# Attention and expert layer on one core: the weights and rows of the left-over steps

## The chip, the cores and the metric

The kernel runs on one core of a Trainium2 chip. The metric is device time in microseconds (us), the median of the timed runs. TensorE (PE) multiplies, ScalarE (ACT), VectorE (DVE) and GpSimd (POOL) do the elementwise work, and SyncE (SP) issues most of the transfers; POOL issues the gathers and scatters of single rows.

## The reference, cut to what matters

```python
# attention: q 4 x 12288 x 128; kv pooled 4x4 into 768 keys per batch, k = v
a = softmax(q @ k.T / sqrt(C));  x = a @ v
# expert layer over all 49152 rows, 8 experts, 128 -> 1024 -> 128
logits = x @ w_gate;  e = argmax(logits);  g = softmax(logits)[e]
y = g * (relu(x @ w1[e]) @ w2[e])
```

Every row goes through the one expert that its gate picks.

## The kernel before, in words

The rows are cut into 96 blocks of 512. Neighbouring blocks form groups, and each group picks by vote the expert that most of its rows want; its blocks then run through that expert in full. Rows whose expert is another one are left over. They are done again at the end in left-over steps of 128 rows (`TAIL`), one expert and one batch to a step. Two such steps (`EXTRA`) are laid out at compile time; a loop on the device (line 1476) takes any that are still missing, and here it runs no time.

A block's expert layer runs in eight parts f of 128 hidden units. `hidden(job, f)` makes three matmuls into one of three PSUM banks m, ACT writes the high half hh (line 549, Relu) and DVE the low half hl (line 555); a bank is free again when hl is there. `combine(job, f)` adds three matmuls with w2 into a bank y, three parts behind (`DEEP`). When a block is done, ACT copies y out as 16-bit planes (line 588), a transposing transfer turns them, and POOL joins and scales them (lines 594 and 598).

Most of the kernel is ordered by hand (`by_hand`). From the last eight blocks on a planner orders the instructions: of those that are ready on an engine by its model it takes the one that stands earliest in the program. `pin` keeps an instruction from passing those that the program has before it on its engine.

In that last stage each part f of a block is followed by one call of `search()`, which advances each left-over step by one piece, up to its next `yield`. Such a stretch is a slice here. The pieces of `tail_step`, in order: the loads of the expert's raw weights, of the batch's keys, values and units (piece 3); finding the 128 rows (pieces 3 to 7); gathering their q (piece 8, line 928, POOL); the maxima of the two raw weights in `weight_scales` (line 495) and their spread over the partitions by a small matmul; then `split_expert` for each weight: wh on ACT (line 523), the raw weight scaled in place on ACT (line 525), wl = raw - wh in two halves on POOL (line 528). Then q's rows are scaled, turned on PE (line 947) and halved (lines 344 and 345), and `scores` makes the six score matmuls, the row maximum (line 361), the exponentials (line 368), their high half (line 391), their low half (line 393, POOL) and a transposing transfer into aT (line 394, SP). After a number of empty pieces `values` multiplies aT with the values (18 matmuls, the first pinned), x is halved (lines 404 and 409), and the gate gives the rows' factors (`scale`). The second step begins one slice after the first has set `found`, which is when its scales are there.

Counted in slices from the first step's start, before the change the first step has its scores in slice 18, its exponentials' transfer in 19 and its values in 28. It sets `found` in 12, so the second step has the same pieces twelve slices later: scores in 30, transfer in 31, values in 40. Slices 1 to 40 are the eight parts each of blocks 91 to 95; what is left after 40 has no part of a block between.

The two steps then run as one last job of 256 rows. Each part f has matmuls for either step; their sums lie in two banks of one tile s. `tail_rows` scales both in one instruction (line 991) and scatters each step's rows with an indirect transfer from POOL (line 994).

Of the kernel before, what the change touches and what calls it, by code (L numbers as in the profile page):

```python
# [13 lines left out]
BF16 = mybir.dt.bfloat16  # L14
I32 = mybir.dt.int32
U16 = mybir.dt.uint16
AF = mybir.ActivationFunctionType
ALU = mybir.AluOpType
AX = mybir.AxisListType

P = 128
# [13 lines left out]
TAIL = 128  # L35
# [5 lines left out]
def attention_moe(ctx: ExitStack, tc, q, kv, w_sr, w_gate, w1, w2, out, tail=True):  # L41
    nc = tc.nc
    B, N, C = q.shape
    H, W = kv.shape[1], kv.shape[2]
    E, F = w_gate.shape[1], w1.shape[2]
    NF = F // P
# [17 lines left out]
    NL = B * E  # L64
    BANKS = 3
    DEEP = 3
    LAG = NBG + 4
    WIDE = LAG + 1
    NJ = NBLK * CH
    TC = TAIL // P  # L70
    assert TC == 1 and NJ * P == B * N
    scale = 1.0 / math.sqrt(C)
# [23 lines left out]
    part = persist.tile([P, 1], F32, name="part")  # L96
# [24 lines left out]
    one = sb.enter_context(tc.tile_pool(name="one", bufs=1))  # L121
    two = sb.enter_context(tc.tile_pool(name="two", bufs=2))
    four = sb.enter_context(tc.tile_pool(name="four", bufs=4))
    three = sb.enter_context(tc.tile_pool(name="three", bufs=3))
    xp = sb.enter_context(tc.tile_pool(name="xp", bufs=LAG))
    EXPERTS = {name: sb.enter_context(tc.tile_pool(name=f"ps_{name}", bufs=1, space=bass.MemoryType.PSUM))
# [19 lines left out]
    def mm(o, l, r, start, stop):  # L146
        return nc.tensor.matmul(o, l, r, start=start, stop=stop)  # L147
# [25 lines left out]
    def pin(ins):  # L173

        return ins if by_hand[0] else tc.keep_in_program_order(ins)
# [160 lines left out]
    def q_tiles(wide):  # L336
        if wide:
            return *(four.tile([P, BLK], F32R, name="qh") for _ in range(2)), None
        qhl = four.tile([P, 2, BLK], F16, name="qh")
        return qhl[:, 0], qhl[:, 1], None  # L340

    def q_halves(qT, n, low, qs=None):
        qh, ql, units = q_tiles(qs is None)
        nc.scalar.copy(qh[:, :n * P], qT[:, :n * P])
        low.tensor_sub(ql[:, :n * P], qT[:, :n * P], qh[:, :n * P])
        return qh, ql, units if qs is None else [qs[:, 1, c:c + 1] for c in range(n)]
# [139 lines left out]
        yield  # L486
        nc.vector.reciprocal(gt, gt)

    def weight_scales(raw, to, where):

        ws = one.tile([P, 8], F32, name="ws", bufs=3)
        wm = one.tile([P, 2], BF16, name="wm", bufs=3)
        to.append(ws)
        for i in range(2):
            pin(nc.vector.tensor_reduce(
                wm[:, i:i + 1], raw[i], axis=AX.X, op=ALU.max, apply_absolute_value=True))
            yield
        pw = where()
        pin(mm(pw[:, :2], ones_q, wm, True, True))
        yield  # L500

        pow2(ws[:, 2:4], pw[:, :2])
        nc.vector.reciprocal(ws[:, 4:6], ws[:, 2:4])
        nc.vector.tensor_scalar_mul(ws[:, 4:5], ws[:, 4:5], W1_TOP / Q_TOP)
        nc.vector.tensor_scalar(ws[:, 6:7], ws[:, 2:3], ws[:, 3:4], Q_TOP / W1_TOP, op0=ALU.mult, op1=ALU.mult)
# [6 lines left out]
                          w2[bass.ds(reg, 1)].rearrange("o (f p) c -> p (o f) c", p=P))  # L512
        return r1, r2

    def split_expert(raw, ws, w, i, aside):

        if aside:
            wh, wl = (kvp.tile([P, F], F16, name="kv_raw") for _ in range(2))
        else:
            wh = two.tile([P, F], F16, name=("w1h", "w2h")[i])  # L520
            wl = two.tile([P, F], F16, name=("w1l", "w2l")[i])
        w += [wh, wl]
        nc.scalar.activation(wh, raw[i], AF.Copy, scale=ws[:, 4 + i:5 + i])
        yield
        nc.scalar.activation(raw[i], raw[i], AF.Copy, scale=ws[:, 4 + i:5 + i])
        yield
        for s in (slice(0, F // 2), slice(F // 2, F)):
            nc.gpsimd.tensor_sub(wl[:, s], raw[i][:, s], wh[:, s])

    def job_parts(job):  # L530

        parts = job.get("parts", [job])
        n = job["n"] // len(parts)
        return [(part, slice(i * n, (i + 1) * n), n) for i, part in enumerate(parts)]
# [11 lines left out]
    def hidden_high(job, f):  # L546
        n, (ph,) = job["n"], job["h"][f]
        hh = one.tile([P, BLK], F16, name="hh", bufs=DEEP + 2)
        nc.scalar.activation(hh[:, :n], ph[:, :n], AF.Relu)  # L549
        job["h"][f] = [ph, hh]  # L550

    def hidden_low(job, f):
        n, (ph, hh) = job["n"], job["h"][f]
        hl = one.tile([P, BLK], F16, name="hl", bufs=DEEP + 2)
        nc.vector.scalar_tensor_tensor(hl[:, :n], ph[:, :n], 0.0, hh[:, :n], op0=ALU.max, op1=ALU.subtract)  # L555
# [4 lines left out]
        hidden_high(job, f)  # L560
        hidden_low(job, f)

    def combine(job, f):
        h = job["h"].pop(f)
        fs = slice(f * P, (f + 1) * P)
        for i, (part, cs, n) in enumerate(job_parts(job)):
            w = part["w"]
            if n == TAIL:
                py = job["py"][:, i, :C] if "parts" in job else job["py"][:, :C]
                mm(py, h[0][:, cs], w[2][:, fs], f == 0, False)  # L570
                mm(py, h[1][:, cs], w[2][:, fs], False, False)
                mm(py, h[0][:, cs], w[3][:, fs], False, f == NF - 1)
                continue
            py = job["py"][:, :n]
            mm(py, w[2][:, fs], h[0][:, cs], f == 0, False)
            mm(py, w[2][:, fs], h[1][:, cs], False, False)
            mm(py, w[3][:, fs], h[0][:, cs], False, f == NF - 1)
# [224 lines left out]
    def moe_step(job, f, last):  # L802

        if f < DEEP and last:
            finish(last, f, f + 1)
        hidden(job, f)

        late = {} if "parts" in job else {DEEP: (), DEEP + 1: (0, 1)}
        for i in late.get(f, (f - DEEP,) if f >= DEEP else ()):
            moe_second(job, i)  # L810

    def moe_second(job, f):
        if f == 0:
            job["py"] = SCORES["s"].tile([P, 2, 512], F32, name="s") if "parts" in job else (
                EXPERTS["y"].tile([P, 512], F32, name="y"))
        combine(job, f)

    def finish(job, lo=0, hi=DEEP):
        for f in range(NF - DEEP + lo, NF - DEEP + hi):
            moe_second(job, f)  # L820
        if hi == DEEP and job["n"] == BLK and all(job is not j for j in jobs[-2:]):
            job["yT"] = y_planes(job["py"])
        elif hi == DEEP and job["n"] == BLK:
            job["y"] = y_out(job)
# [55 lines left out]
    def tail_step(job, place, aside=False):  # L880
# [7 lines left out]
        raw = load_expert(reg_e)  # L888
# [43 lines left out]
        yield  # L932
        w = job["w"] = []
        to = []
        for _ in weight_scales(raw, to, bank):
            yield
        ws = to[0]
        job["found"] = True
        for i in range(2):
            for _ in split_expert(raw, ws, w, i, aside):  # L940
                yield
        qs = q_rows(q_sb, TC)
        q_unit_scores(qs, k)
# [2 lines left out]
        for c in range(TC):  # L946
            pin(nc.tensor.transpose(pq[:, c * P:(c + 1) * P], q_sb[:, c, :], ident))
        qhl = q_halves(pq, TC, nc.vector, qs)
        yield
        sums = one.tile([P, TC], F32, name="sums_t", bufs=2)  # L950
        aT = three.tile([P, 2 * KT, BLK], F16, name="aT")
        for c in range(TC):
            s = scores(qhl, c, k, sums[:, c:c + 1], aT)
# [4 lines left out]
            for _ in s:  # L958
                pass
            yield  # L960
        for _ in range(8):
            yield
        po = bank()
        for t in range(KT):
# [6 lines left out]
        to = []  # L971
# [3 lines left out]
        rs, _, gt, _ = to  # L975
# [9 lines left out]
            next(s, None)  # L985

    def tail_rows(job):
        n = job["n"] // TAIL
        o = two.tile([P, CH, C], F32, name="o")
        py = job["py"][:, :n, :C] if "parts" in job else job["py"][:, :C].unsqueeze(1)  # L990
        nc.vector.tensor_tensor(o[:, :n], py, job["scale"].unsqueeze(2).to_broadcast([P, n, C]), op=ALU.mult)
        writes = []
        for i, part in enumerate(job.get("parts", [job])):
            writes.append(nc.gpsimd.indirect_dma_start(  # L994
                out=out, out_offset=bass.IndirectOffsetOnAxis(ap=part["row"], axis=0),
                in_=o[:, i, :], in_offset=None, bounds_check=B * N - 1, oob_is_err=False).ins)
        for i, write in enumerate(writes):
            for before in writes[:i]:
                tc.declare_no_dep(write, before, reason="a token is in one step alone: the rows are others")
# [114 lines left out]
    jobs = [BL[m] if isinstance(m, int) else m for m in order]  # L1114
# [21 lines left out]
    LEN, SHORT = 18.7, 9.8  # L1136
    FIRST = LAG * (LEN - SHORT)
    events, count = [], [0]

    def at(time, part, *args):  # L1140
        heapq.heappush(events, (time, count[0], part, args))
        count[0] += 1
# [9 lines left out]
    def begin(t):  # L1152
        return FIRST + t * SHORT if t < LAG else t * LEN

# [33 lines left out]
    def plan_short(t):  # L1188

        T, z, y = begin(t), t - 2, t - 3  # L1190
        by_pe = t < LAG - 1
        for c, time in enumerate((0.0, 2.55, 6.05, 8.55)):
# [12 lines left out]
        if z >= 0:  # L1205

            last = t == LAG - 1
            at(T + 4.75, block_values, z, range(0, 2))
# [141 lines left out]
    with tc.manual_schedule():  # L1350
# [12 lines left out]
        for t in range(LAG, NBLK):  # L1363
            m, z, T = t - LAG, t - 2, t * LEN
            job, last = jobs[m], jobs[m - 1] if m else None
# [59 lines left out]
    for t in range(NBLK, LAG + len(jobs)):  # L1425
# [36 lines left out]
        if votes is not None and tail and closes(NBLK - 1) == votes:  # L1462
# [3 lines left out]
                job["to"] = jobs[-1]["scale"][:, i * TC:(i + 1) * TC]  # L1466
            places = tail_places(steps_f[:, :EXTRA], EXTRA)
            waiting += [(job, tail_step(job, places[i], aside=i > 0)) for i, job in enumerate(extra)]
    finish(jobs[-1])
    write_rows(order[-1])  # L1470
    if not tail:
        return
# [3 lines left out]
    with tc.For_i(0, n_steps, 1):  # L1476
        job = dict(n=TAIL)
# [32 lines left out]
```

## Time and profile before

| | us |
|---|---|
| median of 3 timed runs | 1863.18 (1863.13 to 1863.6) |
| the profiled execution | 1862.85 |
| its span, first to last instruction | 1861.1 |

| engine | busy us | share of the span |
|---|---|---|
| PE | 1820.6 | 98% |
| DVE | 1438.9 | 77% |
| POOL | 1392.6 | 75% |
| ACT | 1375.9 | 74% |

Busy times are sums over the span; a matmul's end is modelled, so that neighbouring matmuls overlap in the rows. Idle time stands in square brackets behind the instruction that it precedes, with what ended it.

### The profile page before, as it was taken

What the parts mean: (1) busy time and instruction counts of PE and PEld (TensorE: products, weight loads), DVE (VectorE), ACT (ScalarE), POOL (GpSimd) and SP (SyncE); (2) the same over time, 40 slices, a digit from 0 to 9 for tenths busy, and PEclk for the clock granted to TensorE, in tenths of its full rate; (3) what the DMA queues carried; (4) which work ended last, traced back from release to release, by engine and by line L of the source; (5) the groups of instructions that cost most, each with busy time, mean ns of one, the idle gap of its engine ahead of it and who ended that gap; (6) DMA issues with size and microseconds to landing.
All of it is one profiled execution on the core that took longest, in us unless ns stands there. A gap on an engine that the chain in (4) does not pass through costs nothing. (4 is left out here: it accounts for less than half of the span.)

```text
span 1861.1 us, 30957 instructions
## 1 busy us (share of the span) xinstructions
PE 1820.6 (98%) x9959; PEld 925.2 (50%) x9959; DVE 1438.9 (77%) x3016; ACT 1375.9 (74%) x2432; POOL 1392.6 (75%) x1521
## 2 busy tenths in 40 slices
PE   6999999999999999999999999999999999999998
PEld 6654444444454544444444444544444444444444
DVE  6887877887788787777787878877777677787586
ACT  3777867777877878877777777787777786877665
POOL 2769788778878878778688797787786877777643
PEclk9999999999999999999999999999999999999999
DMA  6988889777988987778878887777787777776552
GB/s 185 175 157 161 185 162 180 156 128 161 192 176 155 184 161 131 154 149 151 166 152 186 161 171 150 140 152 153 131 157 149 131 145 150 138 148 138 97 144 55
DMA packets 994837, 284.74 MB, mean 153 GB/s; under 512 B 900432, under 2 KB 979922, under 8 KB 994672
## 3 DMA queue, kind: packets, MB, share of 16 engines
q1 hardware_dynamic: 994544, 282.65, 77.7%
q8 instruction: 79, 1.29, 0.3%
q14 instruction: 86, 0.70, 0.1%
q0 software_dynamic: 128, 0.10, 0.0%
HBM read 80.42 MB, written 28.45 MB: 59 GB/s over the span
## 5 line engine op out<-in xcount | busy, mean ns | idle before, releaser
L393 POOL TENSOR_TENSOR ah<-a,ah 128x768 f16<-128x768 f32 x379 | 622.2, 1649 | 184.5 <-ACT ah L391 137.6
L549 ACT ACTIVATE hh<-m 128x512 f16<-128x512 f32 x776 | 459.5, 593 | 353.7 <-PE m L147 349.3
L555 DVE SCALAR_TENSOR_TENSOR hl<-m,hh 128x512 f16<-128x512 f32 x776 | 526.9, 680 | 166.3 <-ACT hh L549 160.0
L147 PE MATMUL s<-k_sb,qh 128*128 128x384 f16 (+1 forms) x2316 | 448.1, 329 | 10.0 <-ACT a L368 6.9
L361 DVE TENSOR_REDUCE nmax<-s 128x1 f32<-128x768 f32 x386 | 367.8, 953 | 41.9 <-PE s L147 28.7
L368 ACT ACTIVATE a<-s,nmax,qs 128x768 f32<-128x768 f32 x348 | 346.7, 996 | 49.7 <-DVE qs L152 21.2
L147 PE MATMUL m<-aT,v_sb 128*128 128x512 f16 x1584 | 370.6, 379 | 0.0
L147 PE MATMUL m<-xh,w1h 128*128 128x512 f16 x776 | 292.1, 376 | 3.4 <-DVE hl L555 3.4
L147 PEld LDWEIGHTS <-qh 128*128 128x128 f16 x2100 | 205.3, 98 | 175.6 <-DVE qs L152 3.9
L147 PE MATMUL m<-xh,w1l 128*128 128x512 f16 x776 | 292.5, 377 | 0.0
L147 PE MATMUL m<-xl,w1h 128*128 128x512 f16 x776 | 292.4, 377 | 0.0
L147 PE MATMUL y<-hh,w2h 128*128 128x512 f16 x768 | 290.8, 379 | 0.7 <-ACT y L588 0.7
L147 PE MATMUL y<-hl,w2h 128*128 128x512 f16 x768 | 291.1, 379 | 0.3 <-DVE hl L555 0.3
L147 PE MATMUL y<-hh,w2l 128*128 128x512 f16 x768 | 291.1, 379 | 0.0
L147 PEld LDWEIGHTS <-v_sb 128*128 128x128 f16 x1764 | 169.9, 98 | 201.9 <-issue 1.8
L147 PEld LDWEIGHTS <-w2h 128*128 128x128 f16 x1536 | 149.5, 98 | 180.4 <-issue 1.0
L147 PEld LDWEIGHTS <-w1h 128*128 128x128 f16 x1552 | 135.4, 97 | 120.7 <-issue 12.2
L389 POOL CAST ah<-a 128x768 f16<-128x768 f32 x185 | 152.7, 826 | 48.6 <-ACT a L368 46.4
L391 ACT CAST ah<-a 128x768 f16<-128x768 f32 x194 | 161.8, 834 | 2.0
L594 POOL COPY o<-yT 128x512 uint16<-128x512 uint16 x190 | 136.3, 764 | 33.8 <-DMA yT<-y 33.7
L409 DVE SCALAR_TENSOR_TENSOR xl<-m,xs,xh 128x512 f16<-128x512 f32 x88 | 66.1, 751 | 116.8 <-ACT xh L404 115.3
L653 POOL TENSOR_TENSOR qh<-qT,qh 128x512 f16<-128x512 f32 (+1 forms) x95 | 111.2, 1170 | 31.2 <-ACT qh L648 31.1
(252 smaller groups left out, 2044.5 us busy)
## 6 DMA issues: line engine op xcount, KB each, us to landing
kv_raw<-in_moe_w_dram SPq DMA_DIRECT2D x54, 512.0 KB, 4.8
out_dram<-o SPq DMA_DIRECT2D x96, 256.0 KB, 2.4
q_sb<-in_q_dram SPq DMA_DIRECT2D x380, 64.0 KB, 2.5
kv_raw<-in_kv_dram SPq DMA_DIRECT2D x72, 256.0 KB, 4.4
aT<-ah SPq DMA_TRANSPOSE x379, 3.8
aT<-in_kv_dram SPq DMA_DIRECT2D x8, 512.0 KB, 9.3
kv_raw<-in_kv_dram SPq DMA_DIRECT2D x4, 512.0 KB, 5.6
k_dram<-k_sb SPq DMA_DIRECT2D x8, 192.0 KB, 2.7
```

The source lines that it names most:

```text
L147: return nc.tensor.matmul(o, l, r, start=start, stop=stop)
L361: nc.vector.tensor_reduce(nmax, pss[:, :, :KH], axis=AX.XY, op=ALU.max, negate=True)
L368: nc.scalar.activation(a.rearrange("p (h k) -> p h k", h=2), pss[:, :, :KH], AF.Exp, bias=nmax, scale=units[c] if units else 1.0, accum_ou ...
L389: nc.gpsimd.tensor_copy(ah[:, 0], a)
L391: nc.scalar.copy(ah[:, 0], a)
L393: nc.gpsimd.tensor_sub(ah[:, 1], a, ah[:, 0])
L409: nc.vector.scalar_tensor_tensor(xl[:, :n], po[:, :n], k["xs"][:, 0:1], xh[:, :n], op0=ALU.mult, op1=ALU.subtract)
L549: nc.scalar.activation(hh[:, :n], ph[:, :n], AF.Relu)
L555: nc.vector.scalar_tensor_tensor(hl[:, :n], ph[:, :n], 0.0, hh[:, :n], op0=ALU.max, op1=ALU.subtract)
L594: nc.gpsimd.tensor_copy(o.bitcast(U16).rearrange("p c (d i) -> p i c d", i=2)[:, i], yT.rearrange("p (i c) d -> p i c d", i=2)[:, i])
L653: by.tensor_sub(ql, BL[t].pop("qT"), qh)
```

## The change

The maxima of a left-over step's raw weights are taken in four halves of 512 columns, one in a slice, and a small reduction joins them. The raw weights are scaled in place by POOL and no longer by ACT. One empty piece is put between the halving of q and the scores, and the empty pieces between the exponentials and the values go from eight to five. In the last job the parts f from `LATER` = 3 on are added for the first step alone; the second step's five parts follow in `tail_rows`, after the first step's rows are scaled and their scatter is issued.

```diff
-    def weight_scales(raw, to, where):
+    def weight_scales(raw, to, where, pieces=1):
...
+        if pieces > 1:
+            tops = one.tile([P, 2, 2], BF16, name="wm_tops", bufs=2)
+            for i in range(2):
+                for s in range(2):
+                    pin(nc.vector.tensor_reduce(tops[:, i, s:s + 1], raw[i][:, s * F // 2:(s + 1) * F // 2],
+                                                axis=AX.X, op=ALU.max, apply_absolute_value=True))
+                    yield
+            pin(nc.vector.tensor_reduce(wm, tops, axis=AX.X, op=ALU.max))
...
-        nc.scalar.activation(raw[i], raw[i], AF.Copy, scale=ws[:, 4 + i:5 + i])
+        if by_pool:
+            nc.gpsimd.tensor_scalar(raw[i], raw[i], ws[:, 4 + i:5 + i], None, op0=ALU.mult)
+        else:
+            nc.scalar.activation(raw[i], raw[i], AF.Copy, scale=ws[:, 4 + i:5 + i])
...
-    def combine(job, f):
-        h = job["h"].pop(f)
+    def combine(job, f, only=None):
+        h = job["h"][f] if only == 0 else job["h"].pop(f)
...
+            if only is not None and i != only:
+                continue
...
-        combine(job, f)
+        combine(job, f, 0 if "parts" in job and f >= LATER else None)
...
-        for _ in weight_scales(raw, to, bank):
+        for _ in weight_scales(raw, to, bank, 2):
...
-            for _ in split_expert(raw, ws, w, i, aside):
+            for _ in split_expert(raw, ws, w, i, aside, True):
...
         qhl = q_halves(pq, TC, nc.vector, qs)
+        yield
         yield
...
-        for _ in range(8):
+        for _ in range(5):
             yield
...
-        nc.vector.tensor_tensor(o[:, :n], py, job["scale"].unsqueeze(2).to_broadcast([P, n, C]), op=ALU.mult)
         writes = []
-        for i, part in enumerate(job.get("parts", [job])):
+        for i, part in enumerate(parts):
+            if len(parts) > 1:
+                for f in range(LATER if i else NF - DEEP, NF):
+                    combine(job, f, i)
+            py = job["py"][:, i, :C] if len(parts) > 1 else job["py"][:, :C]
+            nc.vector.tensor_scalar(o[:, i], py, job["scale"][:, i:i + 1], None, op0=ALU.mult)
...
-    finish(jobs[-1])
+    if not tail:
+        finish(jobs[-1])
```

By the pieces, the first step now has its scores in slice 21, the transfer in 22 and its values in 28 as before. It sets `found` in 14, so the second step has its scores in 35, the transfer in 36 and its values in 42, which is behind the same part of block 95 as slice 40.

## Rows read from the trace of the kernel before

**Rows 1.** The first line of the page, the span.

```profile
span 1861.1 us, 30957 instructions
```

**Rows 2.** The table of stretches: start and end, length, then busy us and instructions of PE, PE's weight loads, DVE, ACT and POOL, the granted clock, the DMA share and GB/s. Two stretches in which the left-over steps are prepared.

```profile
1780.00:1800.00 20.00, 17.82 (x81) 7.86 (x80) 18.62 (x42) 13.64 (x22) 10.20 (x11) 1.00 0.93 269
1800.00:1820.00 20.00, 19.07 (x89) 8.56 (x89) 17.49 (x40) 14.00 (x24) 11.74 (x13) 1.00 0.19 42
```

**Rows 3.** Who PE waited for between 1770 us and the end: total us, times, the longest.

```profile
PE m L147 <- DVE hl L555: 1.7, 3, 0.9
PE n L147 <- DVE wm L495: 0.8, 1, 0.8
PE y L147 <- ACT y L588: 0.7, 1, 0.7
PE s L147 <- ACT qh L344: 0.4, 1, 0.4
PE y L147 <- DVE hl L555: 0.3, 1, 0.3
```

**Rows 4.** PE's timeline, two parts of block 92: start, length, instruction, idle time before it.

```profile
1798.59 0.38 PE L147 MATMUL m<-xh,w1h 128*128 128x512 f16 x1 [0.23 <-DVE hl L555]
...
1800.31 0.38 PE L147 MATMUL m<-xh,w1h 128*128 128x512 f16 x1 [0.91 <-DVE hl L555]
```

**Rows 5.** DVE's timeline: a shorter reduction, then the first step's weight maxima.

```profile
1793.55 0.54 DVE L923 TENSOR_REDUCE v<-row 128x1 f32<-128x384 f32 x1
...
1797.88 0.66 DVE L555 SCALAR_TENSOR_TENSOR hl<-m,hh 128x512 f16<-128x512 f32 x1
1798.46 1.21 DVE L495 TENSOR_REDUCE wm<-kv_raw 128x1 bf16<-128x1024 f32 x1
1799.59 0.67 DVE L555 SCALAR_TENSOR_TENSOR hl<-m,hh 128x512 f16<-128x512 f32 x1
1800.18 1.21 DVE L495 TENSOR_REDUCE wm<-kv_raw 128x1 bf16<-128x1024 f32 x1
```

**Rows 6.** ACT's timeline while the second step's first weight is split and block 93's sums are copied out.

```profile
1823.84 1.14 ACT L525 ACTIVATE kv_raw<-kv_raw,ws 128x1024 f32<-128x1024 f32 x1
1824.88 0.57 ACT L588 COPY y<-y 128x512 uint16<-128x512 uint16 x1
```

**Rows 7.** POOL's instructions by line and form: count, busy us, mean ns of one, idle time before. A cast, and one line of TENSOR_SCALAR at two widths.

```profile
L389 POOL CAST ah<-a 128x768 f16<-128x768 f32 x185 | 152.7, 826 | 48.6 <-ACT a L368 46.4
...
L471 POOL TENSOR_SCALAR gate_d<-gate_d 128x128 f32<-128x128 f32 x21 | 11.3, 537 | 1.9
...
L471 POOL TENSOR_SCALAR gate_d<-gate_d 128x64 f32<-128x64 f32 x1 | 0.4, 378 | 0.1
```

**Rows 8.** Timelines of POOL and DVE: two instructions of DVE that lie beside work on POOL, and the same line of DVE earlier, beside none.

```profile
1807.53 2.27 POOL L528 TENSOR_TENSOR w1l<-kv_raw,w1h 128x512 f16<-128x512 f32 x2 [2.98 <-ACT kv_raw L525]
```

```profile
1790.46 0.29 DVE L913 TENSOR_SCALAR sel<-slot,v 128x128 f32<-128x128 f32 x1
...
1807.68 1.09 DVE L913 TENSOR_SCALAR sel<-slot,v 128x128 f32<-128x128 f32 x1
1808.80 1.14 DVE L914 SCALAR_TENSOR_TENSOR sel<-slot,v,sel 128x128 f32<-128x128 f32 x1
```

**Rows 9.** The second step from its scores to its values, from the timelines of PE, DVE, POOL and SP; the row at 1836.85 is part 2 of block 95. Then the time from issue to landing of the two transfers into aT (least, median, most).

```profile
1831.51 0.98 PE L147 MATMUL s<-k_sb,qh 128*128 128x384 f16 x5
...
1836.85 0.38 PE L147 MATMUL m<-xh,w1h 128*128 128x512 f16 x1
...
1844.08 1.17 PE L147 MATMUL n<-aT,v_sb 128*128 128x128 f16 x18
```

```profile
1833.31 0.94 DVE L361 TENSOR_REDUCE nmax<-s 128x1 f32<-128x768 f32 x1
```

```profile
1837.06 1.64 POOL L393 TENSOR_TENSOR ah<-a,ah 128x768 f16<-128x768 f32 x1 [3.69 <-ACT ah L391]
```

```profile
1838.73 1.44 SPq L394 DMA_TRANSPOSE aT<-ah  x1
```

```profile
DMA to landing us min/median/max: 3.7/3.7/3.7
```

**Rows 10.** The same transfer and the values of the first step, and ahead of them what POOL ran before that step's low half.

```profile
1817.03 1.08 POOL L928 DMA_INDIRECT q_sb<-in_q_dram,at  x1
1818.14 1.65 POOL L393 TENSOR_TENSOR ah<-a,ah 128x768 f16<-128x768 f32 x1
```

```profile
1819.81 1.43 SPq L394 DMA_TRANSPOSE aT<-ah  x1
```

```profile
1824.53 1.17 PE L147 MATMUL n<-aT,v_sb 128*128 128x128 f16 x18
```

**Rows 11.** The timeline of the end: the second step's x, the last low half of the last job, the scaling and the two scatters.

```profile
1845.69 0.35 DVE L409 SCALAR_TENSOR_TENSOR xl<-n,xs,xh 128x128 f16<-128x128 f32 x1 [0.73 <-ACT xh L404]
...
1852.40 0.42 DVE L555 SCALAR_TENSOR_TENSOR hl<-m,hh 128x256 f16<-128x256 f32 x1 [0.25 <-ACT hh L549]
...
1853.43 0.42 DVE L991 TENSOR_TENSOR o<-s,scales_t 128x256 f32<-128x256 f32 x1 [0.60 <-PE s L147]
1854.94 1.07 POOL L994 DMA_INDIRECT out_dram<-o,at  x1 [8.72 <-DVEq L1476]
1856.32 0.99 POOL L994 DMA_INDIRECT out_dram<-o,at  x1 [0.30 <-POOLq L1476]
```

More of the change, by code (lines that the diff above doesn't have):

```diff
@@ L66, in attention_moe @@
     DEEP = 3
+    LATER = NF - DEEP - 2
     LAG = NBG + 4
@@ L493, in weight_scales @@
         to.append(ws)
[L494 to L497, printed above, removed]
+        if pieces > 1:
[7 more added lines that the diff above has]
+        else:
+            for i in range(2):
+                pin(nc.vector.tensor_reduce(
+                    wm[:, i:i + 1], raw[i], axis=AX.X, op=ALU.max, apply_absolute_value=True))
+                yield
         pw = where()
@@ L513, in load_expert, with split_expert @@
         return r1, r2
-    def split_expert(raw, ws, w, i, aside):
+    def split_expert(raw, ws, w, i, aside, by_pool=False):
         if aside:
@@ L524, in split_expert @@
         yield
-        nc.scalar.activation(raw[i], raw[i], AF.Copy, scale=ws[:, 4 + i:5 + i])
+        if by_pool:
+            nc.gpsimd.tensor_scalar(raw[i], raw[i], ws[:, 4 + i:5 + i], None, op0=ALU.mult)
+        else:
+            nc.scalar.activation(raw[i], raw[i], AF.Copy, scale=ws[:, 4 + i:5 + i])
         yield
@@ L948, in tail_step @@
         qhl = q_halves(pq, TC, nc.vector, qs)
+        yield
         yield
@@ L987, in tail_rows @@
     def tail_rows(job):
-        n = job["n"] // TAIL
+        parts = job.get("parts", [job])
         o = two.tile([P, CH, C], F32, name="o")
-        py = job["py"][:, :n, :C] if "parts" in job else job["py"][:, :C].unsqueeze(1)
-        nc.vector.tensor_tensor(o[:, :n], py, job["scale"].unsqueeze(2).to_broadcast([P, n, C]), op=ALU.mult)
         writes = []
-        for i, part in enumerate(job.get("parts", [job])):
+        for i, part in enumerate(parts):
[4 more added lines that the diff above has]
+            nc.vector.tensor_scalar(o[:, i], py, job["scale"][:, i:i + 1], None, op0=ALU.mult)
             writes.append(nc.gpsimd.indirect_dma_start(
```

## The prediction

> **What bounds the kernel now.** I read the page's first line, then the table of stretches, then who PE waited for, and last the timelines of the few places that these name. The span is 1861.1 us [rows 1] of the profiled execution's 1862.85; the median is 1863.18, 0.33 above it, so I make the sum against 1862.85 and add 0.33 at the end. PE is the bound nearly everywhere, and the change touches nothing of the hand-ordered part: it can win only what PE loses while the left-over steps are prepared, and what lies behind PE's last matmul. In the two stretches of 20 us from 1780 on PE is busy 17.82 and 19.07 us, and DVE comes close behind it with 18.62 and 17.49 [rows 2]. From 1770 us to the end PE's waits add up to 1.7 + 0.8 + 0.7 + 0.4 + 0.3 = 3.9 us [rows 3]. That is 0.21% of the time: the whole prize of the middle is about one measurement's worth (a difference under 0.2%, 3.7 us, can't be told from none here).
>
> **Maxima in halves.** Two stalls of PE, 0.23 and 0.91 us, stand before parts 3 and 4 of block 92, both for hl [rows 4]. On DVE the two hl are followed each by a maximum of 1.21 us [rows 5], so that a slice costs DVE 0.6 + 1.13 us start to start where PE needs 6 x 0.216 = 1.3. A half of 512 columns is 0.67 us, worked out from 0.54 at 384 and 1.21 at 1024 [rows 5]. Then a slice costs 0.6 + 0.67, about what PE needs. The first hl still comes when it does (1797.88), so 0.23 stays; the second comes 0.54 earlier, so 0.91 becomes 0.37. Gain 0.54; the bounds are 0 and 1.14. DVE's work grows by 4 x 0.67 + 0.15 - 2 x 1.21 = 0.4 us a step, in slices that now hold room for it. The joining reduction has no row; I give it 0.15, at most the 0.54 of the 384-column one.
>
> **Scores a slice later.** PE stood 0.4 us for qh and 0.3 for an hl right behind [rows 3]. With a slice between, the first goes: gain 0.36, bounds 0 and 0.62.
>
> **Raw weights on POOL.** ACT loses four instructions of 1.14 us [rows 6]. PE's 0.7 us for the copy of y [rows 3] came from this: the scaling of 1823.84 holds ACT until 1824.88, where the copy starts [rows 6]. Gain 0.68, bounds 0 and 0.68, as wh of the other weight stays on ACT and now falls four slices later, among other parts. On POOL no row shows a scaling of 1024 columns. The cast of 768 columns takes 0.826 us, which gives 1.1 at 1024; TENSOR_SCALAR grows by (537 - 378)/64 = 2.5 ns a column, which gives 2.8 [rows 7]. I take 1.2: one input and a wide row, as the cast; 2.8 comes from rows too narrow to carry far. POOL has the room (busy 10.20 and 11.74 of each 20 us [rows 2]), and wl is needed only by the last job, so POOL's time itself is worth nothing. What counts is DVE: the select instruction of line 913 takes 0.29 us beside an idle POOL and 1.09 beside POOL's subtraction, and the next, of line 914, 1.14; they end at 1808.77 and 1809.94, about where the two subtractions (1807.53 + 2.27 for both) end [rows 8]. Longer work on POOL catches more such instructions, with hl queued behind them. I price this at +0.3, bounds -0.3 (the subtractions move off lines 913 and 914) and +4 (below). The Trainium skill's page "SBUF — State Buffer" (Who interferes with whom) says that DVE's second port pair is GpSimd's only one, locked for a whole instruction, and that reductions on DVE never contend; the trace agrees (1.09 us against 0.29), and by that page the halves themselves are safe and the new POOL work is not. The Trainium skill's "GPSIMD Engine Reference" (Engine selection) holds one-input work there to be about as fast as on VectorE, which no row here shows at this size; it speaks for 1.1, and the sum would be the same.
>
> **The exponentials come late.** The five empty pieces and the later start of the second step move its scores from slice 30 to 35 while its values stay behind part 7 of block 95. Before, its last scores ended at 1832.49, its transfer was issued at 1838.73 and landed 3.7 us later, at 1842.4; PE came to the values at 1844.08 [rows 9]. The slack is 1.7 us. Slice 35 lies behind part 2 of block 95, three matmuls from 1836.85 [rows 9], so 1837.5 on the old clock; since the scores (1.14 us) no longer stand ahead of that, they start at 1836.4 and end at 1837.5, 5.0 us later than before. All gains above shift this and the values alike. The chain behind the scores was 6.24 us to the issue; 0.8 of it was DVE coming late to the maximum (1833.31) [rows 9], so 5.4 to 6.2. Landing is then at 1846.6 to 1847.4, and PE waits 2.5 to 3.4 us. Some of this is filled: nine matmuls of block 95's last sums, its four turns and the first step's share of the hidden parts don't need these values. What they fill shortens the rest: from the second step's xl (1845.69 + 0.35) to the last hl (ends 1852.82) it is 6.8 us [rows 11], of which some 1.0 is such work. Net +1.9 us, bounds +0.5 (the planner puts the scores a slice earlier) and +3.4 (nothing filled). The first step's scores move three slices, 3 x 1.3 - 1.1 = 2.8 us. Its transfer landed at 1823.5 and PE came at 1824.53, a slack of 1.0; POOL held its low half back until the gather's end (1817.03 + 1.08) [rows 10], which now may cost nothing. So +0 to +1.8; I take +0.4, since PE has a block's work that the planner can put ahead.
>
> **The end.** Now the last hl ends at 1852.82, the common scaling at 1853.85, and the first scatter starts at 1854.94, 1.09 us after it; the second 1.38 after the first [rows 11]. After, part 7 has three fewer matmuls ahead (0.17 us), and only three, not six, stand between the last hl and the first scaling, of half the width: 0.44 against 0.61 until it starts, and some 0.32 against 0.42 in length (between half and the whole). So the first scatter starts 0.17 + 0.17 + 0.10 = 0.44 us earlier and the second follows 1.38 later, since the second scaling (15 matmuls at some 0.055 from start to start, then 0.32) is done about 1.0 us after the first. Gain 0.44. Bounds 0, if the scatter's start hangs on the loop that the row names as its releaser (DVE's queue, line 1476), and 0.7.
>
> **The sum.** -0.54 - 0.36 - 0.68 + 0.3 + 1.9 + 0.4 - 0.44 = +0.6: 1862.85 + 0.6 = 1863.45 for an execution like the profiled one, 1863.8 for the median. All best ends give -1.14 - 0.62 - 0.68 - 0.3 + 0.5 - 0.7 = -2.9; all worst ends +4 + 3.4 + 1.8 = +9.2.
>
> **Rivals.** First, the late exponentials cost nothing: the planner takes the scores early and fills the gap. The lateness terms go, and the sum is -1.7: 1861.5. For it: only the values' first matmul is pinned, and DVE has idle time before hl there. Against it: PE has no idle time in which to take the scores early. Second, slower: DVE is held by POOL. If a raw scaling takes 2.8 us [rows 7] and one of DVE's instructions with two SBUF inputs meets it near its start in three of the four, each holds hl back by up to 2.8; three banks cover some 1.3 of this, so 3 x 1.5 = 4.5 us, and with the rest 1863.8 + 4.2 = 1868.0. It decides from about 2.3 us a scaling. It is the lock of the skill's SBUF page, here as lines 913 and 914 show it. Against it: the cast, and four small chances. Third, the values block PE in full, for both steps (+3.4 and +1.8 in place of +1.9 and +0.4): 1863.8 + 2.9 = 1866.7. Fourth, the scatter doesn't move, as the loop's semaphores release it: +0.44, 1864.2.
>
> **How the numbers follow.** The forecast 0.54 (1862 to 1865.7), the first rival 0.22, the second 0.09, the third 0.09, the fourth 0.06. Faster by over 0.2% (under 1859.5) would need more than all gains together: 0.03, for a luckier order out of the planner, taken from the first rival. Slower by over 0.2% (over 1866.9): the second rival and a third of the third, 0.11. Within: 0.86. The range leaves out the lower half of the first rival and the upper ends: 1861.2 to 1866.8.
>
> **What the profile after would show.** Right: four reductions of about 0.67 us a step on DVE; the waits before block 92's parts 3 and 4 down to about 0.6; none for the copy of y; POOL's TENSOR_SCALAR of 1024 columns at 1.1 to 1.3 us; the second step's transfer landing after PE could have used it, with 2 to 3 us of waiting, or filler, before its values; two scalings of 128 columns and the first scatter some 0.4 us sooner after the last hl. Wrong: no wait at the values (then the first rival), instructions of DVE of over 1.5 us beside the raw scaling (the second), or stalls elsewhere from another order of the planner, which I can't see from here.

## The result, and the profile after

| | median us | range of the runs |
|---|---|---|
| before | 1863.39 | 1863.13 to 1865.64, 4 runs |
| after | 1874.97 | 1873.45 to 1876.46, 4 runs |

The ratio is 1.0058, with a 95% interval of 1.0046 to 1.007: the change makes the kernel slower, by some 11 us. The forecast was 1863.8, its range ended at 1866.8, and slower had a chance of 0.11.

The page of after begins with its span, 10.6 us longer than before [rows 1]:

```profile
span 1871.7 us, 30969 instructions
```

Who PE waited for between 1770 us and the end, after (total us, times, the longest; waits under 0.5 left out):

```profile
PE m L148 <- DVE hl L568: 5.7, 5, 3.8
PE n L148 <- DMA aT<-ah: 3.2, 1, 3.2
PE n L148 <- DVE sel L929: 1.5, 1, 1.5
PE y L148 <- DVE hl L568: 1.0, 1, 1.0
PE n L148 <- DVE wm L505: 0.8, 1, 0.8
PE s L148 <- DVE o L1012: 0.5, 1, 0.5
```

These come to 12.7 us, against 3.9 [rows 3]. To see where the time came in, the end is cut at three marks that every trace has: ACT's copies of block 91's and of block 94's sums, and the last hl's end. The table of stretches gives the granted clock behind the busy times; first before, then after, each from the copy of block 91 to that of block 94, and from there to the last hl:

```profile
1797.75:1837.40 39.65, 37.18 (x187) 17.00 (x186) 32.15 (x82) 29.33 (x51) 21.89 (x22) 1.00 0.26 62
1837.40:1852.80 15.40, 15.39 (x156) 10.28 (x153) 10.59 (x29) 8.25 (x20) 3.78 (x4) 1.00 0.30 63
```

```profile
1797.00:1841.50 44.50, 36.88 (x179) 16.85 (x178) 32.52 (x84) 23.71 (x44) 27.86 (x22) 0.96 0.22 53
1841.50:1864.00 22.50, 19.06 (x152) 12.67 (x151) 11.31 (x33) 10.13 (x23) 9.23 (x8) 0.85 0.22 54
```

The first stretch is 4.9 us longer, the second 7.0 by its marks (1837.37 to 1852.82, and 1841.49 to 1863.90). In the first PE's idle time (length less busy) goes from 2.5 to 7.6 us. In the second it goes from nothing to 3.4, and PE is busy 3.7 us longer as well, at a mean granted clock of 0.85. What lies behind the last hl is 1.0 us shorter, and some twelve times as much is lost ahead of it.

**The first stretch.** DVE's timeline of after shows what stands where the whole maxima stood [rows 5]:

```profile
1797.87 0.67 DVE L499 TENSOR_REDUCE wm_tops<-kv_raw 128x1 bf16<-128x512 f32 x1
1801.67 0.29 DVE L331 TENSOR_REDUCE qs_rows<-q_sb 128x1 f32<-128x128 f32 x1 [3.13 <-DMA q_sb<-in_q_dram,at]
1801.87 0.68 DVE L568 SCALAR_TENSOR_TENSOR hl<-m,hh 128x512 f16<-128x512 f32 x1
```

The half takes the 0.67 us that the prediction gave it. But behind the first half the planner has put the reduction over the gathered q rows (`q_rows`, line 331), ahead of the hl. It waits 3.13 us for the gather, DVE works in order, and the hl that frees a bank for PE stands behind it. POOL issues the gather at 1798.50, behind its subtractions, and the trace gives 3.1 us from its issue to its landing (2.5 for the second step's gather):

```profile
1795.39 2.92 POOL L541 TENSOR_TENSOR w2l<-kv_raw,w2h 128x512 f16<-128x512 f32 x2
1798.50 1.27 POOL L943 DMA_INDIRECT q_sb<-in_q_dram,at  x1 [0.19 <-issue]
```

```profile
DMA to landing us min/median/max: 3.1/3.1/3.1
```

In before the same reduction stands behind both maxima [rows 5] and waits for nothing; POOL's row of the gather there, its time to landing and DVE's row:

```profile
1799.09 1.25 POOL L928 DMA_INDIRECT q_sb<-in_q_dram,at  x1 [0.19 <-issue]
```

```profile
DMA to landing us min/median/max: 3.4/3.4/3.4
```

```profile
1803.31 0.28 DVE L330 TENSOR_REDUCE qs_rows<-q_sb 128x1 f32<-128x128 f32 x1
```

PE's timeline behind that, and two later stalls, of after:

```profile
1802.61 0.58 PE L148 MATMUL m<-xh,w1h 128*128 128x512 f16 x1 [3.80 <-DVE hl L568]
1802.98 0.63 PE L148 MATMUL m<-xl,w1h 128*128 128x512 f16 x1
...
1805.47 0.38 PE L148 MATMUL y<-hl,w2h 128*128 128x512 f16 x1
...
1816.27 0.92 PE L148 MATMUL n<-vT,sel 128*128 128x386 f32 x2 [1.52 <-DVE sel L929]
...
1826.46 0.38 PE L148 MATMUL y<-hl,w2h 128*128 128x512 f16 x1 [0.96 <-DVE hl L568]
```

Where the prediction wanted 0.91 us to fall to 0.37 [rows 4], 3.80 stand. The matmuls right behind come 0.43 us apart, not 0.216: the granted clock is down to the lower of its two levels (1.2 of 2.4 GHz) until some 1805. Two stretches of it:

```profile
1802.50:1805.00 2.50, 2.40 (x6) 0.84 (x6) 2.47 (x7) 0.60 (x1) 1.21 (x2) 0.50 0.08 26
...
1855.00:1857.50 2.50, 2.50 (x22) 1.94 (x20) 0.35 (x1) 0.37 (x1) 0.00 (x0) 0.50 0.02 7
```

**The second stretch.** The second step's scores, 5.9 us ahead of block 94's copy in before [rows 9], now come behind it. After, by PE, POOL and SP:

```profile
1841.94 1.14 PE L148 MATMUL s<-k_sb,qh 128*128 128x384 f16 x6
...
1854.20 2.08 PE L148 MATMUL n<-aT,v_sb 128*128 128x128 f16 x18 [3.19 <-DMA aT<-ah]
```

```profile
1848.25 1.04 POOL L613 TENSOR_TENSOR o<-o,cover 128x512 f32<-128x512 f32 x1
1849.25 1.64 POOL L394 TENSOR_TENSOR ah<-a,ah 128x768 f16<-128x768 f32 x1
```

```profile
1850.92 1.40 SPq L395 DMA_TRANSPOSE aT<-ah  x1
```

PE has nothing left from 1851.0 to 1854.20, and then works at half clock until about 1860 (the row at 1855.00 above). A part of the lateness is POOL's queue: the cast ahead of the low half ends at 1847.35, and POOL comes to it at 1849.25.

### The profile page after: what moved, and what is told of

The parts are those of the page before. It is cut to its first block, busy times and chain, and to the rows that moved or that the text cites. A ratio compares the mean times of both kernels' runs of the same rounds, so it can differ in the third digit from the quotient of the medians.

```text
span 1871.7 us, 30969 instructions
## 1 busy us (share of the span) xinstructions
PE 1826.7 (98%) x9959; PEld 929.8 (50%) x9959; DVE 1440.4 (77%) x3023; ACT 1373.2 (73%) x2428; POOL 1403.8 (75%) x1525
## 3 DMA queue, kind: packets, MB, share of 16 engines
q8 instruction: 79, 1.29, 0.3%
```

## The experiments

Each compares with runs of the kernel before on the same chip (1864.08, 1863.76 and 1863.99 us in the three sets).

**The four parts, one at a time.** `halves`: the maxima in four halves, one to a piece, and nothing else.

```diff
+            for i in range(2):
+                for s in range(2):
+                    pin(nc.vector.tensor_reduce(tops[:, i, s:s + 1], raw[i][:, s * F // 2:(s + 1) * F // 2], ...
+                    yield
```

> The kernel before with the maxima in halves alone (the empty pieces stay at eight, so that both steps' values come two slices later and the second step's scores four). Theory one, order on DVE: the time that the halves leave on DVE lets the planner queue the reduction over q's rows (line 330) ahead of a low half hl, in both steps; DVE then stands for the landing of the gather, about 3 us and 2.7 us, PE stalls over 3 us at block 92 and runs at half clock for some microseconds behind it: +5 to +8 us, about 1869 to 1871. Theory two, POOL: the loss comes from the raw scaling of 2.85 us on POOL, which is not in this kernel: -0.5 us. Theory three, late exponentials: the second step's scores come four slices later: +1 to +3 us, as a wait at its values.

1872.67 us, ratio 1.0042 (1.0026 to 1.0059). The halves alone bring about three quarters of the loss, a little more than theory one gave them, and the wait that theory three names is there as well: 2.51 us at the second step's values. DVE's timeline of this run shows the same wait for the gather as in after:

```profile
1802.33 0.28 DVE L330 TENSOR_REDUCE qs_rows<-q_sb 128x1 f32<-128x128 f32 x1 [3.26 <-DMA q_sb<-in_q_dram,at]
```

`pool`: the raw weights scaled by POOL, and nothing else.

```diff
-        nc.scalar.activation(raw[i], raw[i], AF.Copy, scale=ws[:, 4 + i:5 + i])
+        nc.gpsimd.tensor_scalar(raw[i], raw[i], ws[:, 4 + i:5 + i], None, op0=ALU.mult)
```

> The kernel before with the raw weights of the left-over steps scaled on POOL alone. Order on DVE: the reduction over q's rows stays where it was, so no change, -0.7 to +0.3 us. POOL: four scalings of 2.85 us hold instructions of DVE with two inputs in SBUF and put the low half of the exponentials behind them: +1.5 to +4 us. Late exponentials: no change.

1863.42 us, ratio 1.0002 (0.9992 to 1.0011). One scaling takes 2.86 us, and still nothing can be measured; the +1.5 to +4 us of the theory about POOL don't come.

`scores`: an empty piece ahead of the scores, seven for eight behind them.

```diff
         qhl = q_halves(pq, TC, nc.vector, qs)
+        yield
         yield
...
-        for _ in range(8):
+        for _ in range(7):
```

> The kernel before with one empty piece ahead of the scores and seven instead of eight behind the exponentials (values in the same slices as before). Order on DVE and POOL: -0.4 us, as PE no longer stands for qh. Late exponentials: one slice of 1.3 us less slack, where 1.7 us were there: within 0.5 us of before.

1863.76 us, ratio 0.9999 (0.9989 to 1.0008). In its trace PE's wait for qh is gone; the first step's values wait 1.11 us for their transfer instead, the second step's wait for nothing.

`end`: the last job's new order alone.

```diff
-        combine(job, f)
+        combine(job, f, 0 if "parts" in job and f >= LATER else None)
...
+            nc.vector.tensor_scalar(o[:, i], py, job["scale"][:, i:i + 1], None, op0=ALU.mult)
```

> The kernel before with the new order of the last sums alone (the first step's rows scaled and scattered while the second's are summed). All theories: the first scatter 0.4 us earlier, -0.4 us; 0 if the scatter hangs on the loop's semaphores.

1864.3 us, ratio 1.0 (0.999 to 1.0009). The first scaling comes where it was expected, but the scatter doesn't follow it. SP's write of the last block's rows and POOL's scatters in this run:

```profile
1852.51 0.37 SPq L850 DMA_DIRECT2D out_dram<-o  x1
```

```profile
1855.78 1.07 POOL L1000 DMA_INDIRECT out_dram<-o,at  x1 [8.77 <-DVE o L999]
1857.15 0.98 POOL L1000 DMA_INDIRECT out_dram<-o,at  x1 [0.30 <-POOLq L1483]
```

The scaling (line 999) is done at 1854.20, 1.58 us ahead of the scatter that the trace puts down to it, so it isn't what was waited for. The scatter starts 3.27 us behind the issue of the write. In before the write is issued at 1851.76 and the scatter starts 3.18 us later [rows 11]. Both go to the same output, which points at the write: the scatter waits until it has landed. The trace of `a_two_pin` below names it. The write's landing itself stands at 2.3 us behind its issue in before and 2.4 in `end`; why the scatter starts only 0.9 us after that stays open.

**The reduction kept in program order.** `halves_pin` is `halves`, `a_pin` is the changed kernel, each with one word more.

```diff
-        nc.vector.tensor_reduce(qs[:, 1, :n], q_sb[:, :n], axis=AX.X, op=ALU.max, apply_absolute_value=True)
+        pin(nc.vector.tensor_reduce(qs[:, 1, :n], q_sb[:, :n], axis=AX.X, op=ALU.max, apply_absolute_value=True))
```

> The kernel before with the maxima in halves and the reduction over q's rows kept in its place. Order on DVE: the 8.6 us that the halves alone cost fall to the wait at the values that four later slices give, +1 to +4 us. If the halves themselves cost the time, it stays at +8.

> The changed kernel, with the reduction over q's rows kept in its place in the program on DVE. Order on DVE: both waits of DVE for the gather go, and with them the stall of 3.8 us, its half clock and the stalls at the second gather (0.96 + 0.55 + 0.38): -5 to -7 us, some 1868 us; what is left over the kernel before is the wait at the second step's values and its half clock. POOL or late exponentials as the main cause: under -2 us.

`halves_pin`: 1868.85 us, ratio 1.0025 (1.0016 to 1.0035). `a_pin`: 1867.51 us, ratio 1.0014 (1.0005 to 1.0024). In the changed kernel the pin takes back 0.44% (from 1.0058), some 8 us, in `halves` 0.17% (from 1.0042), and no wait of DVE for the gather is left. Both are still slower than before; `halves_pin`, 5.1 us above its before, missed its +1 to +4. In `halves_pin` DVE's second step meets POOL's subtractions (POOL is in them from 1807.54 to 1812.03):

```profile
1808.82 1.01 DVE L920 TENSOR_TENSOR v<-v,vT 128x1 f32<-128x1 f32 x1
1809.86 1.14 DVE L922 TENSOR_SCALAR sel<-slot,v 128x128 f32<-128x128 f32 x1
1811.04 1.14 DVE L923 SCALAR_TENSOR_TENSOR sel<-slot,v,sel 128x128 f32<-128x128 f32 x1
```

and PE stands behind them, and again at the second step's values:

```profile
1812.83 0.38 PE L147 MATMUL m<-xh,w1h 128*128 128x512 f16 x1 [3.26 <-DVE hl L564]
...
1851.27 2.08 PE L147 MATMUL n<-aT,v_sb 128*128 128x128 f16 x18 [2.23 <-DMA aT<-ah]
```

**Two guesses at the rest that missed.** `a_pin_act` is `a_pin` with the raw weights scaled by ACT again, to see whether POOL's longer work makes the exponentials late.

```diff
-            for _ in split_expert(raw, ws, w, i, aside, True):
+            for _ in split_expert(raw, ws, w, i, aside):
```

> As the one before, and the raw weights scaled on ACT again. If the wait at the second step's values comes from POOL (the exponentials' low half stood 1.9 us for POOL's queue in the changed kernel), it shrinks by about 1.9 us and the time falls by 2 us more, to some 1866; if it comes from the slices alone, it stays and the time falls by under 0.7 us.

1870.84 us, ratio 1.0035 (1.0022 to 1.0047): slower than `a_pin`, not faster. The wait at the second step's values stays (2.13 us, against 2.12), and a stall of 3.30 behind the selections comes back as in `halves_pin`; the first step's values wait 1.81 us, against 0.75. POOL's scaling is not the cause of the wait at the second step's values.

`a_pin_early` sets `found` with the fourth half, so that the second step starts in the slice that it had before; the extra piece is out, and six empty ones stand ahead of the values.

```diff
-        for _ in weight_scales(raw, to, bank, 2):
+        for n, _ in enumerate(weight_scales(raw, to, bank, 2)):
+            if n == 3:
+                job["found"] = True
             yield
...
-        job["found"] = True
...
-        yield
         yield
...
-        for _ in range(5):
+        for _ in range(6):
             yield
```

> As the first, raw weights on POOL, but the second step begins twelve slices after the first as in the kernel before (found is set with the fourth half), the extra empty piece is gone and six empty pieces stand behind the exponentials, so that its scores come in slice 32 and its values in 40. If the late slices cause the wait at its values, the wait falls by three slices of 1.3 us, to none, and the time is within 1 us of the kernel before, about 1863; if POOL's queue causes it, over 1 us of it stays.

1868.09 us, ratio 1.0024 (1.0014 to 1.0033), missed: 2.07 us of the wait at the second step's values stay. The selections run quickly, but the run doesn't test what it was built for. Counted in PE's timeline, its second step's scores come only one part of block 95 earlier than in after (six parts are left between them and the values, against five), not three. And the first step has only seven parts of a block between its scores and its values, against ten in before and eight in after, so that these wait too:

```profile
1827.55 2.08 PE L148 MATMUL n<-aT,v_sb 128*128 128x128 f16 x18 [3.09 <-DMA aT<-ah]
```

What is left is a theory of the slices: it is not the halves that cost, it is that four of them in four pieces move all that follows two slices later. The rival: the halves themselves upset DVE's order.

**Halves without the slices, slices without the halves.** `halves_two` puts two halves into each piece; `shift` and `shift_pin` keep whole maxima of 1.21 us and put two empty pieces ahead of them, with the reduction free and in program order.

```diff
                     pin(nc.vector.tensor_reduce(tops[:, i, s:s + 1], raw[i][:, s * F // 2:(s + 1) * F // 2],
                                                 axis=AX.X, op=ALU.max, apply_absolute_value=True))
-                    yield
+                yield
```

```diff
+        yield
+        yield
         for _ in weight_scales(raw, to, bank):
             yield
```

> The kernel before with the maxima in halves, but two halves in each piece, so that the work behind the maxima stays in the slices it had; the q rows' reduction is free, as in the run halves. Theory of the slices (what costs is that four halves in four pieces move all that follows two slices later: the second step's selections come beside GpSimd's subtractions, the q reduction comes ahead of a sum's half, the second step's scores come late): no gap of over 1.5 us at TensorE between 1795 and 1835, 1862.8 to 1864.5. Rival (the halves themselves upset VectorE's order): a reduction that waits some 3 us for the gather, as in halves, 1868 or more.

> The same as shift_pin with the q rows' reduction free. Theory of the slices: with two more slices between gather and maxima the planner sets the reduction ahead of the maxima and VectorE waits there for the gather, up to 3.2 us; 1868 to 1873, above shift_pin. If the reduction is set ahead only where halves stand, it is equal to shift_pin.

> The kernel before with whole maxima of 1.21 us, two empty pieces ahead of them, and the q rows' reduction kept in program order: the slices of halves_pin without the halves. Theory of the slices: what halves_pin showed (1868.85, a gap of 3.3 us behind the selections, 2.1 us at the second step's values) comes back without the halves, 1866 to 1870. Rival (the halves themselves): 1863.5 to 1865.

`halves_two`: 1864.66 us, ratio 1.0 (0.9991 to 1.0009). `shift`: 1874.57 us, ratio 1.0054 (1.004 to 1.0068). `shift_pin`: 1868.75 us, ratio 1.0024 (1.0015 to 1.0033). Two empty pieces in the kernel before, which compute nothing, cost what the whole change costs; the halves without them cost nothing. In `shift` the reduction stands ahead of both maxima, and DVE waits longer still:

```profile
1802.33 0.28 DVE L330 TENSOR_REDUCE qs_rows<-q_sb 128x1 f32<-128x128 f32 x1 [3.84 <-DMA q_sb<-in_q_dram,at]
```

With the pin, `shift_pin` has its wait at the second step's values. The gap of 3.3 us behind the selections, which was expected as well, doesn't come: PE's longest wait for an hl there is 1.7 us.

```profile
1852.50 1.17 PE L147 MATMUL n<-aT,v_sb 128*128 128x128 f16 x18 [2.73 <-DMA aT<-ah]
```

**All four parts without the slices.** `a_two_pin` is `a_pin` with two halves in each piece and seven empty pieces for five.

> The changed kernel with two halves in each piece, seven empty pieces ahead of the values for five, and the q rows' reduction kept in program order: all four parts of the change, and the work behind the maxima where it was, but for the scores, one slice later. Theory of the slices: 1862.5 to 1865. If the parts cost together what none costs alone (GpSimd's longer scaling, the scores' slice): 1866 to 1868, as a_pin (1867.5).

1863.43 us, ratio 0.9992 (0.9983 to 1.0001). No wait at the values is left, and no lower clock ahead of the last hl. It is the best of the kernels with the change, but it can't be told from before.

The marks of each trace, in us: copy of block 91's sums to that of block 94's; from there to the last hl's end; from there to the second scatter's end. Some of the second step's work (its scores, 1.14 us, among it) moves from the first column to the second where the step comes late. The last column counts, in PE's timeline, the parts f of a block that run between the second step's scores and its values.

| kernel | to block 94 | to the last hl | to the scatter's end | parts ahead of the values |
|---|---|---|---|---|
| before | 39.6 | 15.5 | 4.5 | 9 |
| after | 44.5 | 22.4 | 3.5 | 5 |
| `halves` | 46.6 | 19.7 | 4.3 | 6 |
| `shift` | 46.5 | 19.4 | 3.8 | 6 |
| `halves_pin` | 40.2 | 21.6 | 3.7 | 3 |
| `shift_pin` | 39.2 | 21.9 | 3.7 | 3 |
| `a_pin` | 38.7 | 20.2 | 3.5 | 5 |
| `halves_two` | 40.7 | 15.5 | 4.3 | 9 |
| `a_two_pin` | 38.0 | 15.4 | 4.6 | 9 |

The pin mends the first column alone. With the work back in its slices both are mended, and without a pin too (`halves_two`). The last column goes with the second: where nine parts run, the values wait for nothing; where three to six run, they wait 2.1 to 3.2 us.

## Why the prediction was wrong

**The step that failed** is "Maxima in halves". It worked out what a slice costs DVE and took the order of everything else for granted; the moved slices were counted for the scores and the values alone. The q reduction, not pinned, stood in no term: the gather's landing and the reduction's place behind the maxima were not looked up, though the prediction says itself that stalls from another order of the planner can't be seen from there. They can be looked for: in before the gather is issued by POOL at 1799.09 and lands 3.4 us later, at 1802.5, and the reduction runs at 1803.31. That is 0.8 us of slack, on an engine that works in order and with no pin on it; two slices more, as `shift` shows without any halves, and the reduction stands ahead of hl. Slack alone doesn't decide it (in `halves_two` 0.3 us are left, and the order holds): the planner's own model does, and what it takes the gather to last was not looked into. Taken back by the pin, this is worth 0.44% in the changed kernel (1.0058 to 1.0014), 0.30% in `shift` (1.0054 to 1.0024) and 0.17% in `halves` (1.0042 to 1.0025).

**"The exponentials come late"** is the second step that failed: the right mechanism, at a third of its price. The wait at the second step's values was put at 2.5 to 3.4 us ahead of any filling, and 3.19 came, but that nearness is luck. PE did fill, some 1.4 us: six of the nine matmuls of block 95's last sums and a hidden part of the first step stand ahead of the wait.

```profile
1848.74 0.38 PE L148 MATMUL y<-hh,w2h 128*128 128x512 f16 x1
...
1850.04 0.22 PE L148 MATMUL m<-xh,w1h 128*128 128x128 f16 x1
...
1850.64 0.38 PE L148 MATMUL y<-hh,w2l 128*128 128x512 f16 x1
```

But from the scores' end to the transfer's issue it took 7.84 us (1843.08 to 1850.92), not 5.4 to 6.2. 1.90 of them are the wait for POOL, whose time was held to be worth nothing; in `a_pin` and `a_pin_act`, with the scaling on POOL and on ACT, that wait is 0.84 and 0.85. And nothing was put down for the clock, which fell behind the wait and stayed at half for some 5 us, which costs about 2.5. The second stretch grew by 7.0 between the marks, of which 3.19 are the wait, 1.14 the scores that moved into it, and about 2.5 the clock. Without the scores that is 5.8, against the term's 1.9 and its upper bound of 3.4. The first step's values didn't wait (+0.4 was forecast). The scores alone a slice later cost nothing (`scores`), and all four parts with that one slice cost nothing either (`a_two_pin`). What makes the second step too late is the halves' pieces: two slices in each step, so four for the second step's scores, while behind slice 40 no part of a block is left to fill the time.

**The scaling on POOL** took the upper bound, 2.85 us, not 1.2: TENSOR_SCALAR's slope of [rows 7] was right and the cast the wrong neighbour. The second rival's condition (2.3 us a scaling) was met, and its price still didn't come: `pool` is at 1.0002. Where POOL does hold DVE, PE stands 1.52 us for the selection in after and 1.29 in `a_two_pin`, which loses nothing that can be measured. The first scaling of after and DVE beside the second (POOL, then DVE):

```profile
1810.09 2.86 POOL L536 TENSOR_SCALAR kv_raw<-kv_raw,ws 128x1024 f32<-128x1024 f32 x1 [6.29 <-ACT w2h L533]
...
1814.17 2.85 POOL L536 TENSOR_SCALAR kv_raw<-kv_raw,ws 128x1024 f32<-128x1024 f32 x1
```

```profile
1814.24 1.12 DVE L928 TENSOR_SCALAR sel<-slot,v 128x128 f32<-128x128 f32 x1
1815.28 0.68 DVE L568 SCALAR_TENSOR_TENSOR hl<-m,hh 128x512 f16<-128x512 f32 x1
1815.88 0.34 DVE L929 SCALAR_TENSOR_TENSOR sel<-slot,v,sel 128x128 f32<-128x128 f32 x1
```

The selection that starts right behind the scaling is held until 1815.36, 1.2 us into it; the next, 1.7 us into the same scaling, takes 0.34, though POOL's next instruction starts only at 1816.98. The Trainium skill's page "SBUF — State Buffer" (Who interferes with whom) holds GpSimd's lock for a whole instruction; by its row here the lock, if it is one, ends well before POOL's 2.85 us do.

**The end.** The forecast was 0.44. The stretch behind the last hl became 1.0 us shorter in the changed kernel, but the total didn't fall measurably where nothing else was late (`end`, `a_two_pin`). The fourth rival was right that the scatter doesn't move, and named the wrong cause: it is the write of the last block's rows, not the loop. In `a_two_pin` the trace says so (SP, then POOL):

```profile
1854.28 0.37 SPq L862 DMA_DIRECT2D out_dram<-o  x1
```

```profile
1857.39 1.10 POOL L1013 DMA_INDIRECT out_dram<-o,at  x1 [9.28 <-DMA out_dram<-o]
```

From issue to scatter: 3.18 us in before, 3.27 in `end`, 3.11 in `a_two_pin`. In after the write is issued at 1861.12 and has landed when the scaling is done, since all else is late. But the new order is the smaller part of the 1.0: `halves_pin` and `shift_pin`, which keep the old order, are 0.8 shorter as well, for the same reason. From the last hl to the first scatter it is 2.12 us in before, 1.31 in these two and 1.07 in after, so the new order is worth 0.24 us there, near the 0.27 of the forecast's 0.44 that lie behind the last hl.

**The gains in the middle** were sized at 0.54 for the halves, 0.36 for the scores and 0.68 for ACT's relief. None could be measured by itself, which was said beforehand. In `a_two_pin` the first stretch is 1.7 us shorter than in before, near their sum of 1.58, but not by the same terms: both waits before parts 3 and 4 are gone although its halves stand in pairs of 1.27 us, and the 1.29 for the selection is new. The whole is at 0.9992, an interval that holds 1.

**The chances.** Slower was given 0.11; its own terms, 0.09 and a third of 0.09, make 0.12, and neither held the reduction over q's rows.

**Left open**: by what the planner takes the reduction for ready ahead of hl; and how much of the rest in `halves_pin` and `a_pin_act` is the second step's selections beside POOL's subtractions. The stalls of 3.26 and 3.30 us stand there, but the first column of `halves_pin` is only 0.6 above before. `shift_pin` has no slow selection and costs the same, so it isn't needed to explain the loss.

## What to carry to other kernels

Where a planner sets the order, an edit that adds pieces is first of all a shift of all that comes behind them: test the shift alone, empty, before pricing what the pieces compute. List every instruction there that waits for a transfer and is not pinned, with its slack in the trace of before, and ask what stands behind it on its engine. And price a wait that leaves PE with nothing not at its length alone, but with the clock behind it.

## What had not been expected of the hardware

The clock behind a stall: after 3.80 and 4.48 us of idle time (after, `shift`) PE went on at the lower level, and after 3.26 (`halves_pin`) it fell to it four matmuls later; after the 1.52 of after and the 0.91 of before it did not in the rows that follow. Around the second step's values it also fell after shorter waits: in `halves_pin` the 18 matmuls behind 2.23 us took 2.08, and in `shift_pin` behind 2.73 us 1.17, with the fall 1.5 us after their start (granted clock 1.00 from 1852.5 to 1853.5, 0.50 from 1854.0). The length of the last wait alone doesn't tell it.

POOL's TENSOR_SCALAR of 1024 float columns takes 2.85 us, while a subtraction of 512 takes 1.16: 2.8 ns a column against 2.3, though it reads one operand and not two. Their outputs differ as well (float32 and float16), so the operands alone aren't compared.
